# Routed attention and MLP on one core: one ordered list of steps, PV and logits with tokens on partitions, batch 0 in two rounds

## The chip, the cores and the metric

The kernel runs on one core of a Trainium2 chip. The core has five engines with instruction streams of their own: TensorE (PE in the profile; its weight loads are PEld), VectorE (DVE), ScalarE (ACT), GpSimd (POOL) and SyncE (SP), and 16 DMA engines which all queues share. The metric is the device time of one execution in microseconds. Every engine takes its instructions in the order in which they are written, so an instruction that waits holds everything behind it on that engine.

## The reference, cut to what matters

```
B, H, S, D = 4, 8, 768, 64            # 16 clusters; MLP 512 -> 2048 -> 512
q_assign = argmax(q_n @ c_n.T)        # q, k and centroids normalized; per head
k_assign = argmax(k_n @ c_n.T)
scores   = q @ k.T / 8, set to -1e9 where q_assign != k_assign
attn     = softmax(scores)            # over keys
x        = (attn @ v), heads side by side: 3072 tokens x 512
h        = x @ w_in                   # 3072 x 2048
out      = (h * sigmoid(h)) @ w_out   # 3072 x 512
```

A token attends only to keys whose nearest centroid is its own. The length of q or k doesn't change its argmax, so only the centroids are normalized in the kernel. Inputs and output are float32.

## The kernel before, in words

One head is one (batch, head) pair, 32 in all. A head passes through these stages:

- **Load** (`load_qk`, `load_v`): q, k and v, 192 KB each, over SP's queue. Token p*6+j lies on partition p, so each partition reads 1536 bytes in one piece.
- **Split** (`hi` L90, `lo` L96, both DVE): q and k times 128 as a float16 high half and a float16 remainder, side by side in `hl`.
- **Turn** (`xpose` L106): one DMA transpose of twelve 128x128 tiles into `ab`: 64 rows of high half and 64 rows of remainder, tokens along the free side.
- **Cluster logits** (`logits` L116): the centroids are the weights, 32 columns wide, `ab` the moving operand, 384 columns; four matmuls for four column groups of the array, and four more for the centroids' remainder.
- **Argmax** (`am_t` L126, `am_max` L133 and L135, `am_back` L142): transposed in 32x32 blocks on DVE, maximum, one-hot, transposed back.
- **Codes** (`codes` L151, L153, DVE): the one-hot, times 16384, is written over 16 of the remainder rows of `ab`, for keys less 16384. A score matmul over 80 rows then adds zero for equal clusters and a large negative number otherwise.
- **Scores** (`qk_mm` L162, L163) and **exponential** (`exp` L169, ACT): per 128 keys two matmuls, 512 and 256 queries, and one exponential over 768 into `P`, keys on partitions.
- **PV** (`pv_mm` L177): v and 64 columns of ones are the weights (`vts`, cast on POOL, L82), `P` the moving operand, 384 queries at a time, summed over six key tiles in `pO`. The result has head dimensions on partitions, and the ones give the softmax denominators on the other 64.
- **Normalize**: `evac` (L186, DVE) copies `pO` to `osb`; the denominators are sent over SP as `zt`, inverted (`recip` L196), sent to DRAM (`rzd`), and read back broadcast over 64 partitions (`rzb`); `norm` (L213, POOL) multiplies into `xts`, the transposed input of the MLP.

The MLP takes half a batch (384 tokens) at a time: 16 up units of four matmuls with `win_s` as weights (`unit_a` L232), tanh on ACT (L236), (tanh+1)*h on DVE (L237); then three down units of 16 matmuls with 512 columns (`unit_b` L271), an output copy (L276, DVE) and a store (L277). It needs x of all eight heads of its batch. The last batch goes through `unit_aa` (L251, L259, L261), where two halves share one bank pair and one tanh.

The order is written out by hand: a loop over heads and six key tiles, in which the work of neighbouring heads stands at fixed places (scores of the next tile, PV and normalizing of the heads before, loads five and six heads ahead). MLP units of the batch before are put between at fixed places, four up units and one down unit per head. The MLP weights come over POOL's queue, one piece every second head from head 2 on, behind a small copy (`pace`). What the last heads leave over runs behind the loop.

Of the kernel before, what the change touches and what calls it, by code (L numbers as in the profile page):

```python
# [14 lines left out]


@with_exitstack
def kernel(
# [19 lines left out]
    NBH = B * H  # L38
    HALF = S // 2
    assert D == 64 and DM == H * D and S == 768 and HC == 16 and H == 8  # L40
# [4 lines left out]
    NV = 8  # L45

    ctx.enter_context(tc.manual_schedule())

    const = ctx.enter_context(tc.tile_pool(name="const", bufs=1))
    drpool = ctx.enter_context(tc.tile_pool(name="drpool", bufs=1, space=bass.MemoryType.DRAM))  # L50
    mp = ctx.enter_context(tc.tile_pool(name="mp", bufs=1))
    ps = ctx.enter_context(tc.tile_pool(name="ps", bufs=1, space=bass.MemoryType.PSUM))
# [3 lines left out]
    xts = [const.tile([128, NT], f16, name=f"xt{r}") for r in range(NR)]  # L56
    vts = [const.tile([128, NJ, 128], f16, name=f"vt{n}") for n in range(NV)]
    stk = const.tile([128, H, 32], f16, name="stk")
    ckl = const.tile([128, H, 32], f16, name="ckl")
    ohp = [const.tile([128, 12, 32], f16, name=f"oh{n}") for n in range(2)]  # L60
    pace = const.tile([128, 1], f32, name="pace")

    nat, hls, abs_, psLs, LTs, mxs, ohs, Ps, pOs, osbs, zts, rzds, rzbs, pst = ({} for _ in range(14))

    def per_head(f):
        return lambda i, *a: f(i, *a) if 0 <= i < NBH else None

    @per_head
    def load_qk(i):
        b, h = divmod(i, H)  # L70
        qk = mp.tile([128, 2, NJ * D], f32, name="qk", bufs=3)
        nc.sync.dma_start(qk[:, 0, :], q[b, h].rearrange("(p j) d -> p (j d)", j=NJ))
        nc.sync.dma_start(qk[:, 1, :], k[b, h].rearrange("(p j) d -> p (j d)", j=NJ))
        nat[i] = qk

    @per_head
    def load_v(i):
        b, h = divmod(i, H)
        vn = mp.tile([128, NJ, D], f32, name="vn", bufs=3)
        nc.sync.dma_start(vn, v[b, h].rearrange("(p j) d -> p j d", j=NJ))  # L80
        lo = 0 if i % 2 == 0 else 64
        nc.gpsimd.tensor_copy(vts[i % NV][:, :, lo : lo + D], vn)  # L82

    @per_head
    def hi(i, t=slice(0, 2)):
        if i not in hls:
            hls[i] = mp.tile([128, 2 * NJ, 2, D], f16, name="hl", bufs=3)
        hl = hls[i].rearrange("p (t j) c d -> p t j c d", t=2)
        src = nat[i].rearrange("p t (j d) -> p t j d", d=D)
        nc.vector.tensor_scalar(out=hl[:, t, :, 0, :], in0=src[:, t], scalar1=QS, scalar2=None, op0=ALU.mult)  # L90

    @per_head
    def lo(i, t=slice(0, 2)):
        hl = hls[i].rearrange("p (t j) c d -> p t j c d", t=2)
        src = nat[i].rearrange("p t (j d) -> p t j d", d=D)
        nc.vector.scalar_tensor_tensor(  # L96
            out=hl[:, t, :, 1, :], in0=src[:, t], scalar=QS, in1=hl[:, t, :, 0, :], op0=ALU.mult, op1=ALU.subtract
        )

    @per_head  # L100
    def xpose(i, parts=1):
        hl = hls.pop(i)
        ab = mp.tile([128, 2 * NJ, 128], f16, name="ab", bufs=5)
        n = 2 * NJ // parts
        for t in range(parts):
            nc.sync.dma_start_transpose(ab[:, t * n : t * n + n, :], hl[:, t * n : t * n + n].rearrange("p n c d -> p (n c d)"))  # L106
        abs_[i] = ab

    @per_head
    def logits(i):  # L110
        h = i % H
        ab = abs_[i]
        psL = ps.tile([128, HALF], f32, name="psL", tag="mm", bufs=3)
        for w, st in ((stk, True), (ckl, False)):
            for g in range(4):
                nc.tensor.matmul(  # L116
                    psL[32 * g : 32 * g + 32, :], w[:, h, :],
                    ab[:, 3 * g : 3 * g + 3, :].rearrange("p n c -> p (n c)"),
                    start=st, stop=not st,
                )  # L120
        psLs[i] = psL

    @per_head
    def am_t(i):
        LT = mp.tile([128, 12, 32], f32, name="LT", bufs=2)
        nc.vector.transpose(LT.rearrange("p n c -> p (n c)"), psLs.pop(i))  # L126
        LTs[i] = LT

    @per_head
    def am_max(i):  # L130
        LT = LTs.pop(i)
        mx = mp.tile([128, 12], f32, name="mx", bufs=2)
        nc.vector.tensor_reduce(out=mx, in_=LT[:, :, 0:HC], axis=AX.X, op=ALU.max)  # L133
        oh = ohp[i % 2]
        nc.vector.tensor_tensor(  # L135
            out=oh[:, :, 0:HC], in0=LT[:, :, 0:HC], in1=mx.unsqueeze(2).to_broadcast([128, 12, HC]), op=ALU.is_ge
        )

    @per_head
    def am_back(i):  # L140
        ohT = mp.tile([128, HALF], f16, name="ohT", bufs=2)
        nc.vector.transpose(ohT, ohp[i % 2].rearrange("p n c -> p (n c)"))  # L142
        ohs[i] = ohT
# [74 lines left out]
    gts = {}  # L218
    late = []

    def flush():
        while late:
            late.pop(0)()
# [281 lines left out]
```

## Time and profile before

| | us |
|---|---|
| median of 3 runs | 397.43 (392.53 to 397.45) |
| the profiled execution's own time, from first instruction to last (its span) | 395.2 |
| PE busy | 334.0 (85%) |
| DVE busy | 264.4 (67%) |
| ACT busy | 203.8 (52%) |
| POOL busy | 99.0 (25%) |
| mean granted TensorE clock | 0.965 of full |

Busy time is time in which an engine has at least one instruction running. For PE it counts the depth of the pipeline too: matmuls overlap, and the distance between their starts tells what one costs. In lists of groups, the columns are line, engine, operation, output and inputs with shapes, count, busy time in us, mean duration of one in ns, and idle time of the engine ahead of it with what ended it. In timelines the first two columns are start and duration in us; a merged entry has its count behind an x. In the 40 slices each digit is a busy share in tenths of 9.88 us.

### The profile page before, as it was taken

Reading aid. Unit: us, or ns where it says so; the run is one execution under the profiler, and the core shown is the slowest. Engines: PE = TensorE matmul, PEld = TensorE weight load, DVE = VectorE, ACT = ScalarE, POOL = GpSimd, SP = SyncE. Lnnn points to the kernel's source line nnn. Section 1 sums busy time; section 2 is a strip of 40 time slices with the busy share of each in tenths; the row PEclk is TensorE's granted clock in tenths of the full one; section 3 lists DMA queues with packets and bytes.
Section 4 is the critical chain, followed back from the end, with each engine's and each line's share of the span. In section 5 each row is a group of like instructions: output and inputs, shape, how many; then the busy total and the mean of one; then the engine's idle time right before and its main releaser. Section 6 shows DMA issues by size and latency. Waiting matters only on the chain.

```text
span 395.2 us, 5664 instructions
## 1 busy us (share of the span) xinstructions
PE 334.0 (85%) x1921; PEld 167.8 (42%) x1921; DVE 264.4 (67%) x590; ACT 203.8 (52%) x310; POOL 99.0 (25%) x148
## 2 busy tenths in 40 slices
PE   0539868977598799997999899979999999977995
PEld 0114433433254455553555455445555545443442
DVE  5959967876479977794788877786766345256421
ACT  4237746854376755573666666555657524044300
POOL 3110135454343222223221402260223105000000
PEclk9999978888599999999999999999999999999999
DMA  5695899999979835572555555544311103200022
GB/s 141 172 269 114 188 202 225 186 213 227 128 138 190 207 87 134 133 176 74 148 147 148 122 148 147 143 85 89 88 48 23 47 27 88 80 2 0 0 81 80
DMA packets 82125, 48.84 MB, mean 124 GB/s; under 512 B 62128, under 2 KB 76464, under 8 KB 82096
## 3 DMA queue, kind: packets, MB, share of 16 engines
q1 hardware_dynamic: 79408, 44.29, 46.6%
q0 software_dynamic: 2688, 4.19, 7.2%
q8 instruction: 15, 0.25, 0.3%
q14 instruction: 14, 0.11, 0.1%
HBM read 33.59 MB, written 6.39 MB: 101 GB/s over the span
## 4 chain that ended last, share of the span: by engine, by line
PE 61%; DVE 15%; DMA 12%; ACT 4%; issue 3%; POOL 2%; SPq 2%; ACTq 0%; POOLq 0%; DVEq 0%
PE po L271 21%; PE ph L232 13%; PE pO L177 12%; PE pS L162 7%; DMA vn<-in_v_dram 4%; PE pS L163 3%; PE phs L251 3%; DMA qk<-in_k_dram 3%; DVE osb L186 2%; DMA rzb<-rzd 2%; DMA zt<-osb 2%; DVE gt L261 2%; DVE gt L237 2%; PE psL L116 2%; DVE hl L90 1%
## 5 line engine op out<-in xcount | busy, mean ns | idle before, releaser
L169 ACT ACTIVATE P<-pS 128x768 f16<-128x768 f32 x192 | 148.1, 809 | 37.4 <-PE pS L163 37.2
L177 PE MATMUL pO<-P,vt 128*128 128x384 f16 x384 | 89.1, 344 | 14.0 <-DVE osb L186 13.9
L236 ACT ACTIVATE tn<-ph 128x384 f32<-128x384 f32 x96 | 47.2, 491 | 101.3 <-PE ph L232 96.2
L162 PE MATMUL pS<-ab 80*128 80x512 f16 x192 | 78.8, 410 | 15.5 <-DVE ab L153 9.2
L232 PE MATMUL ph<-xt,win_s 128*128 128x384 f16 x384 | 78.5, 328 | 9.8 <-POOL xt L213 9.8
L271 PE MATMUL po<-wout_s,gt 128*128 128x512 f16 x384 | 85.7, 379 | 0.0
L213 POOL TENSOR_TENSOR xt<-osb,rzb 64x384 f16<-64x384 f32 x64 | 65.1, 1035 | 49.7 <-DMA rzb<-rzd 48.7
L237 DVE SCALAR_TENSOR_TENSOR gt<-tn,ph 128x384 f16<-128x384 f32 x96 | 53.0, 553 | 35.8 <-ACT tn L236 34.0
L82 POOL CAST vt<-vn 128x384 f16<-128x384 f32 x32 | 18.0, 563 | 180.2 <-DMA vn<-in_v_dram 149.6
L177 PEld LDWEIGHTS <-vt 128*128 128x128 f16 x384 | 37.6, 101 | 58.9 <-issue 39.2
L271 PEld LDWEIGHTS <-gt 128*128 128x128 f16 x384 | 37.5, 98 | 43.6
L163 PE MATMUL pS<-ab 80*128 80x256 f16 x192 | 55.6, 289 | 0.0
L276 DVE TENSOR_SCALAR ot<-po 128x512 f32<-128x512 f32 x24 | 16.6, 692 | 52.3 <-PE po L271 52.3
L232 PEld LDWEIGHTS <-win_s 128*128 128x128 f16 x384 | 37.4, 97 | 26.7 <-issue 1.2
L186 DVE COPY osb<-pO 128x384 f32<-128x384 f32 x64 | 35.3, 551 | 3.2 <-PE pO L177 2.9
L96 DVE SCALAR_TENSOR_TENSOR hl<-qk,hl 128x768 f16<-128x768 f32 (+1 forms) x33 | 33.1, 1002 | 0.2
L162 PEld LDWEIGHTS <-ab 80*128 80x128 f16 x192 | 19.8, 103 | 29.0 <-DVE ab L153 10.3
L163 PEld LDWEIGHTS <-ab 80*128 80x128 f16 x192 | 19.8, 103 | 24.5 <-issue 12.8
L251 PE MATMUL phs<-xt,win_s 128*128 128x384 f16 x128 | 22.2, 327 | 5.2 <-DVE gt L261 5.2
L259 ACT ACTIVATE tn<-phs 128x768 f32<-128x768 f32 x16 | 13.0, 811 | 25.0 <-PE phs L251 25.0
L90 DVE TENSOR_SCALAR hl<-qk 128x768 f16<-128x768 f32 (+1 forms) x33 | 19.1, 580 | 8.7 <-DMA qk<-in_k_dram 5.5
L261 DVE SCALAR_TENSOR_TENSOR gt<-tn,phs 128x384 f16<-128x384 f32 x32 | 16.3, 551 | 12.1 <-ACT tn L259 12.1
(45 smaller groups left out, 175.7 us busy)
## 6 DMA issues: line engine op xcount, KB each, us to landing
qk<-in_q_dram SPq DMA_DIRECT2D x32, 192.0 KB, 3.4
qk<-in_k_dram SPq DMA_DIRECT2D x32, 192.0 KB, 3.2
vn<-in_v_dram SPq DMA_DIRECT2D x32, 192.0 KB, 3.7
rzb<-rzd SPq DMA_DIRECT2D x32, 192.0 KB, 3.9
out_dram<-ot SPq DMA_DIRECT2D x24, 256.0 KB, 2.2
win_s<-in_moe_w_in_dram POOLq DMA_DIRECT2D x4, 512.0 KB, 7.9
wout_s<-in_moe_w_out_dram POOLq DMA_DIRECT2D x4, 512.0 KB, 7.5
ab<-hl SPq DMA_TRANSPOSE x33, 3.8
```

The source lines that it names most:

```text
L96: nc.vector.scalar_tensor_tensor(out=hl[:, t, :, 1, :], in0=src[:, t], scalar=QS, in1=hl[:, t, :, 0, :], op0=ALU.mult, op1=ALU.subtract)
L162: nc.tensor.matmul(pS[:, 0:512], lhsT, ab[0:80, 0:4, :].rearrange("p n c -> p (n c)"), start=True, stop=True)
L163: nc.tensor.matmul(pS[:, 512:768], lhsT, ab[0:80, 4:6, :].rearrange("p n c -> p (n c)"), start=True, stop=True)
L169: nc.scalar.activation(out=P, in_=pst.pop((i, j))[:, 0:S], func=AF.Exp, bias=0.0, scale=ESC)
L177: nc.tensor.matmul(pOs[i], vts[i % NV][:, j, :], Ps[i, j][:, c * HALF : c * HALF + HALF], start=(j == 0), stop=(j == NJ - 1))
L186: nc.vector.tensor_copy(osb[:, c * HALF : c * HALF + HALF], pOs.pop(i))
L213: nc.gpsimd.tensor_tensor(out=xts[h // 2][o : o + 64, b * S + c * HALF : b * S + c * HALF + HALF], in0=osbs[i][o : o + 64, cs], in1=rzbs[i ...
L232: nc.tensor.matmul(ph, win_s[:, r, ts(fb, 128)], xts[r][:, T0 : T0 + HALF], start=(r == 0), stop=(r == NR - 1))
L236: nc.scalar.activation(out=tn, in_=ph, func=AF.Tanh, bias=0.0, scale=0.5)
L237: nc.vector.scalar_tensor_tensor(out=gt[:, fb, :], in0=tn, scalar=1.0, in1=ph, op0=ALU.add, op1=ALU.mult)
L251: nc.tensor.matmul(phs[:, 512 * c : 512 * c + HALF], win_s[:, r, ts(fb, 128)], xts[r][:, T0 : T0 + HALF], start=(r == 0), stop=(r == NR - 1),)
L271: nc.tensor.matmul(po, gt[:, fc, ts(t, 128)], wout_s[:, fc, :], start=(fc == 0), stop=(fc == NFB - 1))
```

## The change

The kernel is rewritten. Every piece of work becomes a step with an engine, an assumed duration, the steps it comes after, the buffers that it uses and a priority. `Plan.order` runs through all steps with the assumed durations, takes at each turn the step that can start first (the lower key where two can), gives out buffers, and so fixes one order; the kernel is then written out in it.

- **PV** (`attention`, `pv`): `P` is the weights, 128 queries at a time, and v the moving operand: 65 columns, 64 of v and a 2.0 whose product is twice the denominator, or 96 for odd heads. A head has 36 such matmuls where it had 12. Queries now lie on partitions, so the reciprocal and the multiply (DVE) read `pO` directly, and `zt`, `rzd`, `rzb`, `evac` and POOL's `norm` are gone. The result `xn` of two heads is turned into `xt` by a DMA transpose, or on PE with a copy on DVE for batch 0's first round and the last pairs of a batch.
- **Logits** (`part`, `logits`): 128 tokens of `ab` are the weights, the centroids (high half and remainder) the moving operand, 96 columns, or twice 16 in batch 0's first round. Tokens lie on partitions, so the argmax needs no first transposition: sum of the parts, maximum, difference, two marks, one transposition.
- **Codes**: four DMA transfers per part from `ohT` into `ab`, 64-byte pieces; on DVE and ACT for the first two parts only.
- **High halves**: on POOL, the very first on ACT.
- **Batch 0**: its K, V and the first half of its Q are loaded and prepared by pairs of heads (first and second pair turned on PE), eight heads of 384 queries run, then the second half of Q, and eight heads of 384 again. The other batches have whole heads. Loads are of two heads in one transfer.
- **MLP**: halves as before, 16 units of one bank each; tanh for one half at a time throughout; output copies on ACT; factors of one half are folded into the 2.0. After the last exponential the four banks of the scores join the MLP's two.
- **Weights**: `win_s` by blocks of 512 columns, each of the eight transfers held back to an assumed time in the plan.
- **Centroids**: the root on POOL with its power function, where ACT's root and two correction steps on DVE stood.

The written order runs all of batch 0's first round ahead of the first up unit, and all 16 up units of the first half ahead of batch 1's first scores; the MLP's steps have the lowest priority and fill what attention leaves.

```diff
-    def logits(i):
-        for w, st in ((stk, True), (ckl, False)):
-            for g in range(4):
-                nc.tensor.matmul(
-                    psL[32 * g : 32 * g + 32, :], w[:, h, :],
-                    ab[:, 3 * g : 3 * g + 3, :].rearrange("p n c -> p (n c)"),
+                    w = T["ab"][A.i][:, a0 + t, :]
+                    if twin:
+                        nc.tensor.matmul(pL[:, HC * t : HC * t + HC], w, stk[:, hh, 0:HC], start=True, stop=False, ...)
+                        nc.tensor.matmul(pL[:, HC * t : HC * t + HC], w, stk[:, hh, HC : 2 * HC], start=False, stop=True, ...)
+                    else:
+                        nc.tensor.matmul(pL[:, 32 * t : 32 * t + WN], w, stk[:, hh, :], start=True, stop=True)
...
-        nc.vector.tensor_scalar(out=dst, in0=ohT[32 * g : 32 * g + HC, :], scalar1=OHV, ...)
+                if place == "DMA":
+                    nc.sync.dma_start(dst, src)
...
-            nc.tensor.matmul(
-                pOs[i], vts[i % NV][:, j, :], Ps[i, j][:, c * HALF : c * HALF + HALF], start=(j == 0), stop=(j == NJ - 1)
-            )
+                    nn = (D + 1) if h % 2 == 0 else WN
+                    nc.tensor.matmul(
+                        pO[:, (D + 1) * t : (D + 1) * t + nn], w, vt[:, VW * j : VW * j + nn],
+                        start=(j == 0), stop=(j == NJ - 1), skip_group_check=True,
+                    )
...
-        nc.sync.dma_start(zt, osb[zr : zr + 1, :].rearrange("o (p c) -> o p c", c=NJ))
-        nc.vector.reciprocal(rz, zts.pop(i))
-        nc.sync.dma_start(rzd.rearrange("(p c) -> p c", c=NJ), rz)
-        nc.sync.dma_start(rzb[o : o + 64, :], rzds.pop(i).unsqueeze(0).to_broadcast([64, S]))
-        nc.gpsimd.tensor_tensor(out=xts[...], in0=osbs[i][...], in1=rzbs[i][...], op=ALU.mult)
+            nc.vector.reciprocal(rz, pO[...][:, :, D])
+            nc.vector.tensor_tensor(out=xn[...], in0=pO[...][:, :, 0:D], in1=rz.to_broadcast(...), op=ALU.mult)
...
+    for place in range(H * (B + 1)):
+        n, h = divmod(place, H)
+        if n == 0:
+            attention(0, h, 0, HJ, 20 * place, "DVE")
+        elif n == 1:
+            attention(0, h, HJ, NJ, 20 * place, "DVE" if h >= 6 else "DMA")
+        else:
+            attention(n - 1, h, 0, NJ, 20 * place, "DVE" if h == H - 1 else "DMA")
+    for b in range(B):
+        mlp(b, 0, 200 * b, lambda t: "ACT")
+        mlp(b, 1, 200 * b + 100, lambda t: "ACT")
+    exps[-1].adds = (pools["M"], [2, 3, 4, 5])
+    for s in plan.order():
+        s.fn()
```

1010 lines of the change are left out of this document (645 added, 365 removed).

## Prediction

> **What bounds the kernel now.** I read the 40 slices first, then busy time by stage.
>
> ```profile
> PE   0539868977598799997999899979999999977995
> DMA  5695899999979835572555555544311103200022
> ```
> ```profile
> core 0: us, PE busy (x) PEld busy (x) DVE busy (x) ACT busy (x) POOL busy (x), PEclk, DMA share, GB/s
> 0.00:50.00 50.00, 27.72 (x157) 11.70 (x157) 39.03 (x97) 25.84 (x35) 9.09 (x24) 1.00 0.74 176
> 50.00:110.00 60.00, 44.52 (x232) 20.73 (x225) 39.53 (x94) 32.09 (x44) 27.61 (x37) 0.77 1.07 199
> 110.00:320.00 210.00, 195.87 (x1199) 103.05 (x1197) 154.47 (x342) 127.48 (x207) 56.41 (x81) 1.00 0.49 117
> 320.00:395.20 75.20, 65.90 (x345) 32.37 (x342) 31.39 (x58) 18.38 (x27) 5.85 (x6) 1.00 0.14 47
> ```
>
> There are two regimes. Until about 110 us the DMA engines are full (share 0.74, then 1.07) and the granted clock is 0.77; afterwards PE is full and DMA is half idle. Busy time overstates PE, because matmuls overlap, so I take what one really costs from the distance between starts in a dense stretch (timeline of PE):
>
> ```profile
> 201.72 0.27 PE L163 MATMUL pS<-ab 80*128 80x256 f16 x1
> 201.93 0.35 PE L116 MATMUL psL<-ab,stk 128*32 128x384 f16 x4
> ...
> 202.37 0.66 PE L177 MATMUL pO<-P,vt 128*128 128x384 f16 x3
> ...
> 203.27 0.81 PE L232 MATMUL ph<-xt,win_s 128*128 128x384 f16 x4
> 203.92 0.65 PE L177 MATMUL pO<-P,vt 128*128 128x384 f16 x3
> 204.41 0.38 PE L162 MATMUL pS<-ab 80*128 80x512 f16 x1
> 204.63 0.27 PE L163 MATMUL pS<-ab 80*128 80x256 f16 x1
> 204.74 3.62 PE L271 MATMUL po<-wout_s,gt 128*128 128x512 f16 x16
> 208.19 0.38 PE L162 MATMUL pS<-ab 80*128 80x512 f16 x1
> ```
>
> From these starts: a 384-column matmul 0.65/4 = 0.162 us (0.42 ns a column), a score pair 0.33, a 512-column one 3.45/16 = 0.216. The eight logits matmuls take 0.65 from 201.72 to 202.37, less 0.11 for the 256 columns ahead of them: 0.54. PE's work is then scores 192 x 0.33 = 63.4, up 512 x 0.162 = 82.9, down 384 x 0.216 = 82.9, PV 384 x 0.162 = 62.2, logits 32 x 0.54 = 17.3: **309 us** of the span of 395.2. So 86 us are idle. Where? These are the first rows (0 to 110) of L162, L177, L232 and L116, by stage:
>
> ```profile
> 0.00:110.00 110.00, 31.97 (x69) 7.93 (x70) 0.88 0.92 189
> 0.00:110.00 110.00, 33.16 (x126) 13.53 (x126) 0.88 0.92 189
> 0.00:110.00 110.00, 3.79 (x12) 1.56 (x12) 0.88 0.92 189
> 0.00:110.00 110.00, 8.54 (x104) 1.95 (x104) 0.88 0.92 189
> ```
>
> 69 x 0.33 + 138 x 0.162 + 13 x 0.54 = 52 us of work in 110: **58 us of the idle time lie there**, since no MLP can run until batch 0 is done. The other 28 are spread over 285 us. What holds batch 0 is in the chain that ended last:
>
> ```profile
> 47.22 7.59 DMA zt<-osb
> ```
>
> A 3 KB transfer took 7.59 us in a full queue, and DVE stood behind it.
>
> **The change part by part.** Counts come from the written order of each engine.
>
> *PE: PV and logits.* 384 PV matmuls of 384 columns become 1152 with P as the weights: 576 of 65 columns, 576 of 96. Logits become 312 of 96 columns and 144 of 16; 70 transposes of 128 columns come in. No row shows such a short pair (load, then matmul), so it is bounded. Below: columns alone, 27, 41 and 7 ns. Above: each 128x128 load hides behind a 0.11 us, 256-column matmul (204.63 to 204.74), so at most 107 ns. Between them:
>
> ```profile
> 201.92 0.10 PEld L116 LDWEIGHTS <-stk 128*32 128x32 f16 x4 [0.32 <-issue]
> ...
> 202.36 0.28 PEld L177 LDWEIGHTS <-vt 128*128 128x128 f16 x3 [0.32 <-issue]
> ```
> ```profile
> L177 PEld LDWEIGHTS <-vt 128*128 128x128 f16 x384 | 37.6, 101 | 58.9 <-issue 39.2 <-POOL xt L213 0.3
> ...
> L116 PEld LDWEIGHTS <-stk 128*32 128x32 f16 x128 | 3.8, 94 | 14.4 <-issue 13.6 <-DVE stk L351 0.7
> ```
>
> Four loads fit into 0.10 us though each lasts 94 ns, and 128 columns last only 7 ns longer than 32. The matmul at 202.37 starts 0.01 after its own load. So most of the 98 ns is latency that overlaps. I take columns plus about 12 to 20 ns: 42 ns (65), 52 (96), 30 (16), 65 (128). Sum: 24.2 + 30.0 + 16.2 + 4.3 + 4.6 = 79 us, against 62.2 + 17.3 = 79.5 now. **PE's work stays at 308 us**; at the bounds it is 22 lower or 101 higher.
>
> The Trainium skill ("TensorE: Matmul & The Clock Gate", Part 3, the paragraph on what overlaps) says that a weight load overlaps running matmuls only when the row group differs. This trace disagrees: L232's loads use all 128 rows, as its matmuls do, and the cadence stays 0.162 us, which is what 384 columns take.
>
> *Denominators.* The chain zt, rzd, rzb (96 transfers, one behind DVE at 47.22), the evacuation and POOL's normalizing go; 40 reciprocals and 40 multiplies on DVE straight from PSUM come.
>
> ```profile
> L213 POOL TENSOR_TENSOR xt<-osb,rzb 64x384 f16<-64x384 f32 x64 | 65.1, 1035 | 49.7 <-DMA rzb<-rzd 48.7
> L186 DVE COPY osb<-pO 128x384 f32<-128x384 f32 x64 | 35.3, 551 | 3.2 <-PE pO L177 2.9
> L153 DVE TENSOR_SCALAR ab<-ohT 16x384 f16<-16x384 f16 x64 | 19.4, 303 | 0.9
> L151 DVE TENSOR_SCALAR ab<-ohT 16x384 f16<-16x384 f16 x64 | 19.0, 297 | 1.5
> L82 POOL CAST vt<-vn 128x384 f16<-128x384 f32 x32 | 18.0, 563 | 180.2 <-DMA vn<-in_v_dram 149.6 <-PE pS L163 24.2 <-PE ph L232 6.5
> L276 DVE TENSOR_SCALAR ot<-po 128x512 f32<-128x512 f32 x24 | 16.6, 692 | 52.3 <-PE po L271 52.3
> L135 DVE TENSOR_TENSOR oh<-LT,mx 128x192 f16<-128x192 f32 x32 | 14.8, 463 | 1.1
> ...
> L196 DVE RECIPROCAL rz<-zt 128x6 f32<-128x6 f32 x32 | 5.9, 184 | 8.0 <-DMA zt<-osb 8.0
> ```
>
> The 384-element multiply lies between 551 ns (L186, same size from PSUM) and 2 x 463 (L135, a broadcast operand); with 0.2 for the reciprocal that is 30 to 45 us on DVE against 35.3 + 5.9 removed: even. *Codes* leave DVE (19.4 + 19.0) for 124 SP transfers. *High halves* go to POOL, two casts of L82's size per head: 32 x 1.13 = 36 us for the 65.1 it loses. *Output copies* (16.6) go to ACT, which has about 190 us free. The argmax gains two short operations, about 0.4 us a head. DVE ends near 230 us, no engine but PE near the span. On SP the codes' issues wait for DVE's transpose, and loads stand behind them; these loads are asked for five places ahead (some 40 us), which hides it.
>
> *Codes on the DMA engines.* 366 tiles x 64 pieces of 64 bytes.
>
> ```profile
> q1 hardware_dynamic: 79408, 44.29, 46.6%
> q0 software_dynamic: 2688, 4.19, 7.2%
> ```
>
> q1's mean packet costs 0.466 x 16 x 395.2 / 79408 = 37 ns; the new ones lie between nothing and that, 0 to 54 us of all engines over the run, for 96 removed transfers with 6 MB of rzb. I take them as even.
>
> *Batch 0 in two rounds.* All K, V and half of Q, then 24 exponentials instead of 48, and the first MLP half can start. In the new order all 64 up-matmuls of that half stand ahead of batch 1's first scores, together with 96 scores, 288 PV, 204 logits matmuls and 49 transposes: 50 us of PE work. Call the time of those scores T.
> ```profile
> 16.14 0.81 ACT L169 ACTIVATE P<-pS 128x768 f16<-128x768 f32 x1 [7.90 <-PE pS L163]
> ```
> ```profile
> L169 ACT ACTIVATE P<-pS 128x768 f16<-128x768 f32 x192 | 148.1, 809 | 37.4 <-PE pS L163 37.2
> ...
> L236 ACT ACTIVATE tn<-ph 128x384 f32<-128x384 f32 x96 | 47.2, 491 | 101.3 <-PE ph L232 96.2 <-DVE gt L237 3.4 <-DVE osb L186 1.1
> ```
> - From below: ACT has 48 exponentials (148.1 / 192 = 0.77 us each), 16 tanh (0.49) and copies of about 3 us, 48 us in all. Its first exponential starts at 16.1 now, and I take 14 (two table loads and the transposes' transit go, POOL's power function comes): T is at least 62.
> - By DMA: weights 7.2% = 28.5 us; q1 46.6% = 184 us, 5.8 a head. About ten heads' worth of traffic stands ahead: 58 + 28.5 = 86 us. The four w_out quarters (14 us) aren't needed by then: 72.
> - From above: 110, as now.
>
> I take **T = 76**. From there PE has 144 score pairs, 864 PV, 252 logits, 196 up, 192 down: 175 us of attention with filler, then 252 up and 192 down with no attention, 83 us.
>
> *Tail.* The up-matmuls of the last batch now wait for their bank:
>
> ```profile
> PE phs L251 <- DVE gt L261: 5.2, 7, 1.0
> ```
> ```profile
> 387.73 3.40 PE L271 MATMUL po<-wout_s,gt 128*128 128x512 f16 x15
> ```
> Six banks instead of two pairs remove that: 5 us, already in the sum since I count the tail at full rate.
>
> **Sum**: 76 + 175 + idle 14 (8% of 175: now 17 of the 210 us from 110 to 320, where PE's work by the same cadences is 193) + 83 + 4 from the last matmul to the end, as now (387.73 + 3.40 to 395.2), = 352 us span. The median of the runs lies 2.2 above the profiled span (397.4 to 395.2), so **354 us**.
>
> **The rivals.**
> 1. *A load holds the array* (slower). If half of a load's 98 ns kept the array from streaming, a pair costs 49 + about 34 = 83 ns, and 1678 pairs cost 139 instead of 79 us: 354 + 60 = 414. At the bound of 107 ns: 455. It overtakes the gain from about 73 ns a pair on. For: no row shows short pairs. Against: four loads in 0.10 us. The Trainium skill ("TensorE: Matmul & The Clock Gate", Back-to-back issue gap) gives about 81 ns for a stream of such pairs at 128 columns; by an estimate from that page 1678 pairs cost 136 us and the time would be about 411.
> 2. *The queue still holds batch 0.* Packets of 64 bytes, a weight stream beside the loads and PE's fixed order, which cannot use filler while a score waits for its codes, keep T at 110: 388. For: 1.07 share now. The Trainium skill ("DMA: Bandwidth & Descriptors", Specifications) wants 512 bytes for line rate, since smaller writes are read and modified first; no row here separates that cost.
> 3. *T is ACT's bound*, 62, and the filler leaves 8 us idle: 334.
> 4. *The two rounds don't do what they say*: POOL issues the weights behind its high halves and casts, w_in arrives late, the first up-matmuls stand at PE's head. Same place and price as 2.
>
> **How the numbers follow.** Forecast (340 to 372) 0.58; rival 3 and better 0.13; rivals 2 and 4 0.15, a third of it within 2% of now; rival 1 0.11, rest 0.03. A difference of 2% (8 us) is about what runs of this kernel, 392.5 to 397.5, can tell. Range: 330 (rival 3 with some of the lower pair bound) to 392 (rival 2). Faster by over 2%: 0.81; within: 0.07; slower: 0.12.
>
> **What would show it.** In the profile after: starts of PV matmuls 40 to 55 ns apart (step 1; 80 or more is rival 1); first up-matmul near 50 us and first score of batch 1 near 76; DMA share below 0.7 after 110 us; granted clock under 0.9 only in the first 80 us; no wait of DVE for a transfer of denominators; some 80 us of MLP alone at the end with PE full; POOL and DVE under 70%. The prediction is wrong if PE stands at scores waiting for codes after 110 us (DMA or DVE late), or if short pairs run over 65 ns.

## The result, and the profile after

The changed kernel takes **380.84 us** (median of 4 runs, 379.38 to 384.62), against 396.48 for the kernel before beside it: a ratio of **0.965, 95% interval 0.958 to 0.973**. It is faster, by 16 us where the forecast of 354 meant 42. The profiled execution's span is 382.6 us, against 395.2. Ratios leave disturbed runs out; for one kernel below (the plan with 3 us) the ratio is therefore lower than its median alone would give.

The 40 slices of the page of after (one slice is 9.57 us), then busy time by stage:

```profile
PE   2740668889989989998798998988999999998995
...
PEclk9955558699999999999899998999999999999999
DMA  7599594289596949548856784838020010100101
```
```profile
core 0: us, PE busy (x) PEld busy (x) DVE busy (x) ACT busy (x) POOL busy (x), PEclk, DMA share, GB/s
0.00:100.00 100.00, 63.30 (x702) 43.98 (x703) 53.01 (x146) 49.73 (x75) 31.51 (x68) 0.76 0.77 153
100.00:292.00 192.00, 174.28 (x1821) 110.94 (x1822) 114.00 (x278) 134.21 (x207) 30.90 (x60) 0.98 0.64 137
292.00:382.60 90.60, 82.70 (x439) 42.49 (x436) 32.00 (x64) 34.01 (x74) 0.00 (x0) 1.00 0.10 35
```

The three stages are batch 0, attention with MLP work between, and the MLP alone. In the first the clock granted to TensorE is 0.76 on average by the row, and 0.5 in slices 3 to 6; the DMA engines are 0.77 busy. In the second the DMA share is 0.64. DVE, which had 264.4 us, has 199.0 by the page, POOL 62.4 instead of 99.0, ACT 217.9 instead of 203.8.

The clock column has a gap: up to the first change that the profile records it counts the clock as full. The distances between starts say otherwise. Timeline of PE in the kernel before:

```profile
30.54 1.17 PE L177 MATMUL pO<-P,vt 128*128 128x384 f16 x3
31.50 0.63 PE L162 MATMUL pS<-ab 80*128 80x512 f16 x1
...
36.11 0.65 PE L177 MATMUL pO<-P,vt 128*128 128x384 f16 x3
36.60 0.38 PE L162 MATMUL pS<-ab 80*128 80x512 f16 x1
```

Three matmuls of 384 columns take 0.96 us at 30.5 us and 0.49 us at 36.1 us: 0.32 and 0.16 us each. So TensorE ran at half pace early in the kernel before, where the page shows 9 in every slice of PEclk up to there and the prediction read a clock of 1.00 for the first 50 us. In after the same happens: transposes of 128 columns start 107 ns apart until 15.6 us and 55 ns apart from 16.9 us on. The 0.76 is therefore too high for the first stage.

**What a short pair costs.** Timeline of PE in after: a run of 16-column logits that alternate between two lines, and three pieces of a dense stretch, all at full clock.

```profile
19.25 0.17 PE L473 MATMUL pL<-stk,ab 128*128 128x16 f16 x1
...
20.13 0.17 PE L477 MATMUL pL<-stk,ab 128*128 128x16 f16 x1
...
114.08 1.71 PE L638 MATMUL pO<-vt,P 128*128 128x96 f16 x36
115.62 0.38 PE L595 MATMUL pS<-ab 80*128 80x512 f16 x1
...
118.33 0.67 PE L482 MATMUL pL<-stk,ab 128*128 128x96 f16 x12
118.84 0.38 PE L595 MATMUL pS<-ab 80*128 80x512 f16 x1
...
122.81 0.89 PE L638 MATMUL pO<-vt,P 128*128 128x65 f16 x24
123.54 0.38 PE L595 MATMUL pS<-ab 80*128 80x512 f16 x1
```

36 pairs of 96 columns take 1.54 us, 43 ns each; 24 of 65 columns 0.73 us, 30 ns; 12 logits 0.51, 42 ns. That is the columns at 0.42 ns and 2 or 3 ns more: every load, though it lasts about 100 ns, is hidden. From the first to the last of 36 matmuls of 16 columns 0.88 us pass, 25 ns each, so going from 65 to 16 columns saves little. All PV and logits matmuls come to 576 x 0.030 + 576 x 0.043 + 312 x 0.042 + 144 x 0.025 = 59 us, and about 5 for the transposes: **64 us** where I had 79.

The Trainium skill ("TensorE: Matmul & The Clock Gate") has two figures for this. Its section "Back-to-back issue gap" gives about 81 ns for a stream of load and matmul pairs at 128 columns; this trace disagrees, with 43 ns at 96, and so does that of the run without weights below, in which twelve transposes of 128 columns start 55 ns apart (20.84 to 21.50 us). Its Part 1 ("Wait — 56ns, not 53.3ns?") says that starts are never closer than about 25 ns however few the columns; the 25 ns here agree.

**The groups that answer to those shown of before** (line, engine, operation, names, shapes, count, busy us, mean ns, idle ahead and what ended it; the second fence keeps shapes apart; the third is the queues' part of the page):

```profile
L638 PE MATMUL pO<-vt,P 128*128 128x96 f16 (+1 forms) x1152 | 56.0, 206 | 1.8 <-ACT P L612 0.9
...
L482 PE MATMUL pL<-stk,ab 128*128 128x96 f16 x312 | 19.0, 212 | 16.7 <-DMA ab<-hl 13.7
...
L651 DVE RECIPROCAL rz<-pO 128x6 f32<-128x6 f32 (+1 forms) x40 | 7.3, 184 | 40.2 <-PE pO L638 39.8
```
```profile
L656 DVE TENSOR_TENSOR xn<-pO,rz 128x384 f16<-128x384 f32 x24 | 13.4, 558 | 0.8
```
```profile
q1 hardware_dynamic: 96848, 40.05, 46.9%
q0 software_dynamic: 4224, 4.19, 6.8%
```

DVE no longer waits for a transfer of denominators: the reciprocal waits for PE. But the logits now wait, and for the DMA transposes: 13.7 us. In the chain that ended last, these transposes have the largest single share:

```profile
DMA ab<-hl 16%; PE pM L745 10%; PE pS L745 9%; PE pM L716 7%; PE pO L638 6%; PE pS L716 6%; PE pS L595 4%; PE pL L482 4%; DMA nv<-in_v_dram 4%; SPq L430 3%; SPq L555 3%; DVE gq L727 3%; DVE hl L417 3%; PE pS L599 2%; ACT P L612 1%
```

The waits (engine, tile and line, what it waited for: total, times, longest):

```profile
ACT P L614 <- PE pS L605: 39.9, 21, 22.7
...
PE pL L482 <- DMA ab<-hl: 13.7, 13, 3.0
PE pL L473 <- DMA ab<-hl: 13.6, 1, 13.6
...
PE pS L745 <- ACT ot L758: 2.7, 4, 0.7
```

The same for PE alone, from 100 to 292 us:

```profile
PE pL L482 <- DMA ab<-hl: 9.0, 11, 2.0
```

One stop of 13.6 us in batch 0, two more (4.6 us) in its second round, and eleven of at most 2.0 us (9.0 in all) behind it. The big one, by the timelines of POOL, SP, PE and ACT:

```profile
18.34 3.20 POOL L774 DMA_DIRECT2D win_s<-in_moe_w_in_dram  x4
...
19.66 18.08 SPq L430 DMA_TRANSPOSE ab<-hl  x2
...
37.85 0.19 PE L473 MATMUL pL<-stk,ab 128*128 128x16 f16 x1 [13.59 <-DMA ab<-hl]
...
44.45 1.51 ACT L614 ACTIVATE P<-pS 128x768 f16<-128x768 f32 x2 [22.72 <-PE pS L605]
```
```profile
20.00:60.00 40.00, 18.16 (x196) 12.10 (x193) 12.11 (x34) 9.61 (x13) 6.57 (x11) 0.50 0.99 152
```

The four w_in pieces are issued from 18.3 us on, and the transposes of batch 0's third and fourth pairs from 19.7 on. SP is held by these two for 18.08 us; PE's next instruction in its order is a logits matmul on their result; ACT gets no score for 22.7 us. From 20 to 60 us the DMA share is 0.99 and the clock 0.50. The first up-matmul and the first scores of batch 1 come accordingly:

```profile
74.72 1.05 PE L716 MATMUL pM<-xt,win_s 128*128 128x384 f16 x5
...
99.95 0.38 PE L595 MATMUL pS<-ab 80*128 80x512 f16 x1
```

So T, the time of batch 1's first scores, is **100.0** instead of 76.

**The balance.** I took every matmul of the trace at its columns and 2 ns as work, and the rest of the distance to the next start as idle (a stretch at half clock counts as half idle):

| | forecast | measured |
|---|---|---|
| T | 76 | 100.0 (43 work, the rest idle or lost to the clock) |
| work from T to the end of attention | 175 | 163 |
| idle there | 14 | 29 (14 of it ahead of logits, L482, whatever they waited for; 5 ahead of up-matmuls, L716) |
| MLP alone, work | 83 | 81 |
| MLP alone, idle | 0 | 5.5 |
| last matmul to the end | 4 | 4 |
| span | 352 | 382.6 |

PE's work is 43 + 163 + 81 = 287 us, where before it was 309; idle time is 382.6 - 287 = 96, where before it was 86. **What the change gained is about 22 us of matmul work, which I had called even; the idle time, which I had expected to shrink, grew by 10.**

### The profile page after: what moved, and what is told of

It reads as the page before. It is cut to its first block, busy times and chain, and to the rows that moved or that the text cites. A ratio compares the mean times of both kernels' runs of the same rounds, so it can differ in the third digit from the quotient of the medians.

```text
span 382.6 us, 7732 instructions
## 1 busy us (share of the span) xinstructions
PE 320.3 (84%) x2958; PEld 197.4 (52%) x2958; DVE 199.0 (52%) x486; ACT 217.9 (57%) x355; POOL 62.4 (16%) x128
## 3 DMA queue, kind: packets, MB, share of 16 engines
q1 hardware_dynamic: 96848, 40.05, 46.9%
## 4 chain that ended last, share of the span: by engine, by line
PE 49%; DMA 22%; DVE 11%; SPq 7%; ACT 4%; issue 3%; POOL 2%; DVEq 0%; POOLq 0%; ACTq 0%
DMA ab<-hl 16%; PE pM L745 10%; PE pS L745 9%; PE pM L716 7%; PE pO L638 6%; PE pS L716 6%; PE pS L595 4%; PE pL L482 4%; DMA nv<-in_v_dram 4%; SPq L430 3%; SPq L555 3%; DVE gq L727 3%; DVE hl L417 3%; PE pS L599 2%; ACT P L612 1%
## 5 line engine op out<-in xcount | busy, mean ns | idle before, releaser
L716 PE MATMUL pM<-xt,win_s 128*128 128x384 f16 x352 | 69.0, 329 | 4.3 <-DVE gq L727 4.3
L716 PEld LDWEIGHTS <-win_s 128*128 128x128 f16 x512 | 50.2, 98 | 41.0 <-issue 8.6
L745 PEld LDWEIGHTS <-gq 128*128 128x128 f16 x384 | 37.6, 98 | 46.4 <-issue 7.0
L727 DVE SCALAR_TENSOR_TENSOR gq<-tn,pM 128x384 f16<-128x384 f32 x88 | 46.0, 545 | 29.8 <-ACT tn L722 29.7
L638 PE MATMUL pO<-vt,P 128*128 128x96 f16 (+1 forms) x1152 | 56.0, 206 | 1.8 <-ACT P L612 0.9
L745 PE MATMUL pM<-wout_s,gq 128*128 128x512 f16 x224 | 57.0, 383 | 0.4 <-DVE gq L727 0.4
L638 PEld LDWEIGHTS <-P 128*128 128x128 f16 x1152 | 51.9, 102 | 9.5 <-issue 1.5
L722 ACT ACTIVATE tn<-pM 128x384 f32<-128x384 f32 x88 | 41.8, 502 | 5.1 <-PE pM L716 4.7
L745 PE MATMUL pS<-wout_s,gq 128*128 128x512 f16 x160 | 36.0, 379 | 3.9 <-ACT ot L758 2.7
L605 PE MATMUL pS<-ab 80*128 80x384 f16 x96 | 28.1, 412 | 7.5 <-ACT ab L557 2.6
L482 PE MATMUL pL<-stk,ab 128*128 128x96 f16 x312 | 19.0, 212 | 16.7 <-DMA ab<-hl 13.7
L716 PE MATMUL pS<-xt,win_s 128*128 128x384 f16 x160 | 28.6, 326 | 0.3 <-ACT tn L722 0.2
L482 PEld LDWEIGHTS <-ab 128*128 128x128 f16 x312 | 15.7, 101 | 23.4 <-DMA ab<-hl 18.9
```

What stands on the lines that cost most here:

```text
L482: nc.tensor.matmul(pL[:, 32 * t : 32 * t + WN], w, stk[:, hh, :], start=True, stop=True)
L605: nc.tensor.matmul(pS[sb.i][:, 512 * i : 512 * i + HALF], ab[0:80, kt[2 * s + i], :], ab[0:80, qt : qt + HJ, :].rearrange("p n c -> p (n c ...
L638: nc.tensor.matmul(pO[:, (D + 1) * t : (D + 1) * t + nn], w, vt[:, VW * j : VW * j + nn], start=(j == 0), stop=(j == NJ - 1), skip_group_c ...
L716: nc.tensor.matmul(banks[bank.i][:, 0:HALF], win_s[:, r, ts(fb, 128)], T["xt"][xtb[b].i][:, r, T0 : T0 + HALF], start=(r == 0), stop=(r == ...
L722: nc.scalar.activation(out=T["tn"][tn.i], in_=banks[bank.i][:, 0:HALF], func=AF.Tanh, bias=0.0, scale=1.0)
L727: nc.vector.scalar_tensor_tensor(out=T["gq"][g.i][:, fb % 4, :], in0=T["tn"][tn.i], scalar=1.0, in1=banks[bank.i][:, 0:HALF], op0=ALU.add, ...
```

## The experiments

My theory after this trace: two things undid the forecast, both through DMA transposes. The weights and the transposes meet on the DMA engines and stop batch 0; and the plan believes that a transpose can be used too soon, so PE's order has logits standing too early. Rivals: the two rounds themselves cost; PE's work alone sets the time; the chain of batch 0 is long whatever DMA does. Each edit is to the changed kernel unless another is named.

### Weights behind the transposes of pairs three and four

```
+    for s in steps:
+        if s in weights and s.start is not None and not getattr(mark, "gone", False):
+            continue
         s.fn()
...
+        if s is mark:                       # the transposes turns[0, 3, 0]
+            mark.gone = True
+            gate()                          # POOL copy of a piece of their result
+            for w in weights:               # the ones held back
...
```

> Edit: POOL copies one element per partition out of the turned tile of batch 0's fourth pair ahead of the first w_in transfer, so that all eight weight transfers start only when the DMA transposes of pairs three and four have landed; nothing else moves. Theory A (the weight stream takes the DMA engines from these transposes): ACT's stop of 22.7 us before its seventh exponential falls below 10, the two transposes are issued within 8 us instead of 18.1, time falls by 8 to 16 us, to 365 to 373. Rival B (two transposes of 18 tiles are this slow by themselves): the stop stays above 17 us, time within 3 us of 381.

Measured: **381.5 us** (378.9 to 383.2), ratio 0.960 (0.953 to 0.968), T 95.7. Timelines of SP and ACT:

```profile
19.47 5.39 SPq L431 DMA_TRANSPOSE ab<-hl  x2
39.47 8.82 SPq L431 DMA_TRANSPOSE ab<-hl  x2
```
```profile
31.20 1.51 ACT L616 ACTIVATE P<-pS 128x768 f16<-128x768 f32 x2 [9.90 <-PE pS L607]
...
56.24 1.51 ACT L616 ACTIVATE P<-pS 128x768 f16<-128x768 f32 x2 [9.73 <-PE pS L607]
```

The same two transposes hold SP for 5.39 us instead of 18.08, and the stop falls from 22.7 to 9.9 us: the weights were what stretched them. Most of the 9.9 us that are left pass before the first weight transfer is issued, at 27.1 us, so they have another cause. And the next pair of transposes, at 39.5, now runs beside the weights, and a second stop of 9.7 us appears. The stop and the transposes did what theory A said; the time did not, it hardly moves. The Trainium skill ("DMA: Bandwidth & Descriptors", Issuing engines are not separate DMA queues) says that transfers from all queues run on the same 16 engines and interleave; this agrees, since a stream from POOL's queue more than tripled the time of SP's transfers.

### Weights behind the second round's transposes

The same edit with `mark = turns[0, 3, 18][0]` and the copy taken from that part's tile.

> Edit: the same copy, but from the turned tile of the second half of Q of the fourth pair, so the weights start when all DMA transposes of batch 0 have landed. Theory A: the first stop is short as in the run before and the PE waits for second-half transposes (3.2, 1.9, 1.9 us) shrink too, but the up-matmuls wait for w_in: the first one no earlier than 10 us after the copy. Time 360 to 378. Rival B: first stop unchanged at over 17 us, time 385 or more, since the weights come later on top.

Measured: **383.3 us** (380.3 to 384.4), ratio 0.963 (0.956 to 0.970), T 99.4.

```profile
73.52 11.05 SPq L431 DMA_TRANSPOSE ab<-hl  x1
...
92.66 1.51 ACT L616 ACTIVATE P<-pS 128x768 f16<-128x768 f32 x2 [10.21 <-PE pS L607]
```

(The first row is of SP, the second of ACT.) Now a transpose of batch 1 meets the weights: 11.05 us for one. The first stop is again about 10 us (10.29), long before the weights, which are issued from 54.9 us on. The time lies above the theory's 360 to 378. The lengthened stop follows the weights to wherever they are put, as long as a DMA transpose is needed soon.

### No weights

```
-                nc.gpsimd.dma_start(
-                    win_s[:, :, ts(n, 512)], moe_w_in.rearrange(...)[:, :, ts(n, 512)]
-                )
+                nc.gpsimd.memset(win_s[:, :, ts(n, 512)], 0.01)
...
-                nc.gpsimd.dma_start(wout_s[:, 4 * n : 4 * n + 4, :], ...)
+                nc.gpsimd.memset(wout_s[:, 4 * n : 4 * n + 4, :], 0.01)
```

> Edit: the eight weight transfers are replaced by POOL memsets of a constant, so the MLP works with constant weights; all else is the same. It leaves the weights' load out, to price it. Theory A': no stop over 10 us in batch 0, first score of batch 1 at 70 to 80, time 352 to 364 (17 to 29 less than 381). Rival C (PE's half clock and the fixed order cost the time between 45 and 75 us whatever the weights do): first score of batch 1 no earlier than 88, time over 368.

Measured: **370.3 us** (369.3 to 372.3), ratio 0.932 (0.925 to 0.940), T 84.8. Timelines of SP and ACT, and PE's waits:

```profile
20.25 5.42 SPq L430 DMA_TRANSPOSE ab<-hl  x2
```
```profile
33.61 1.51 ACT L614 ACTIVATE P<-pS 128x768 f16<-128x768 f32 x2 [11.53 <-PE pS L605]
```
```profile
PE pL L482 <- DMA ab<-hl: 11.7, 12, 2.4
```

The weights cost this kernel 15 us of T and 11 us of time. Neither expectation is met: the stop is 11.5 us, T lies between the two, and the time is above 368, as rival C said. T is still 9 above the forecast, and the waits of logits for transposes from 100 us on are almost unchanged (8.8 us where they were 9.0): they are the second cause, and it has nothing to do with the weights.

The edit has a cost of its own, here and in the last run without weights. POOL fills four pieces for 7 us where it had issued transfers for 3.2 us, and DVE's marks, ahead of the codes, stand beside the fill (timelines of POOL and DVE in that other run):

```profile
18.19 7.03 POOL L774 MEMSET win_s<- 128x2048 f16 x4
```
```profile
22.54 2.80 DVE L535 TENSOR_SCALAR oh<-Df 128x192 f16<-128x192 f32 x1
...
28.59 0.26 DVE L535 TENSOR_SCALAR oh<-Df 128x192 f16<-128x192 f32 x1
```

The same operation takes 2.80 us beside the fill and 0.26 without it; in the run of this section two of them take 2.75 and 2.25 us. So both runs may price the weights too low, by up to 4.5 and 2.5 us.

### First round of batch 0 turned on PE

```
-            hi_eng="POOL", turn={"k": "ACT", "q": "DVE"} if p == 1 else "DMA", twin=True,
+            hi_eng="POOL", turn={"k": "ACT", "q": "DVE"}, twin=True,
```

> Edit: pairs three and four of batch 0's first round are turned on PE with copies on ACT and DVE, as pair two is; the weight stream is left where it is. Theory A' (the weight stream starves whichever DMA transposes are in flight, and PE's fixed order then stands still): the stop of 22.7 us shrinks to under 9 since nothing there needs a DMA transpose, the second round's transposes still meet the rest of the weights; first score of batch 1 at 82 to 92 instead of 100, time 366 to 376. Rival B' (the sum of all DMA work ahead of that point sets it, 77 us of engine time by the windows, and 7 of it go): first score of batch 1 at 93 to 97, time 375 to 380.

Measured: **377.5 us** (373.6 to 378.4), ratio 0.948 (0.940 to 0.956), T 93.4. PE's waits:

```profile
PE pL L482 <- DMA ab<-hl: 16.4, 15, 5.7
PE pS L605 <- DMA ab<-ohT: 9.8, 2, 9.3
```

The stop at the logits of the first round goes; in its place PE stands 9.3 us for codes, which are DMA transfers too, under the same weights. Two thirds of the stop come back one step later (9.3 of 13.6 us). T and the time both lie in the range of rival B', the sum of DMA work, so this run doesn't decide for the theory. Later runs decide against that rival: with batch 0 turned on PE the DMA engines' share up to T is 0.79 of 83.8 us with the weights and 0.46 of 82.0 without, 66 and 38 us of work for nearly the same T.

### The plan's delay for a transpose

In `Plan.order`, one constant: how long after its transfer a DMA transpose may be used.

```
-                s.end = max(wire[s.eng], t + s.w) + (1000 if turned else 1200)
+                s.end = max(wire[s.eng], t + s.w) + (3000 if turned else 1200)
```

> Edit: the plan assumes 3.0 us instead of 1.0 from the end of a transpose's transfer to its use, so logits matmuls are written later in PE's order. If PE's idle time after 100 us (29 us, half of it ahead of logits) comes from an order that takes transposes for too quick: waits of logits for transposes fall from 13.7 to under 6 us and time by 5 to 10 us. If the waits only move to scores (codes come later too): time within 3 us of 381.

Measured: **364.5 us** (359.7 to 371.0), ratio 0.910 (0.900 to 0.918), T 96.9. PE's waits of the profiled execution (span 357.7):

```profile
PE pL L482 <- DMA ab<-hl: 2.2, 3, 1.5
```

By the constants that stand around this line, the plan had reckoned 0.3 + 12 x 0.195 + 1.0 = 3.6 us from the issue of a 12-tile transpose to its use; the trace of after has a median of 3.9 us to the landing alone, over all of them, and 3.7 to 6.8 us for those of 12 tiles from 100 us on (issues by group: count, us to landing):

```profile
ab<-hl SPq DMA_TRANSPOSE x30, 3.9
```

With the new constant, 13.7 us of waits became 2.2 (from 100 us on, 9.0 became 2.2), and the time from T to the end fell from 282.6 to 260.8 us. By the balance above, idle time after T until attention ends is 15 us instead of 29, and 11 of these 14 lie ahead of logits; the MLP's own stretch has 3.5 us less idle time, and 4.4 us more of matmul work lie before T. The matmuls come to the same 287 us; PE has other work standing ahead of each logits matmul. The gain is above the 5 to 10 us that I expected.

### Both, in all of batch 0

The constant of 3000, the edit of the first round, and the second round's parts turned on PE too:

```
-                0, p, [("q", 0, HJ, NJ), ("q", 1, HJ, NJ)], 18, 40 + 20 * p, hi_eng="POOL", pace=s
+                0, p, [("q", 0, HJ, NJ), ("q", 1, HJ, NJ)], 18, 40 + 20 * p, hi_eng="POOL", turn={"k": "ACT", "q": "DVE"}, pace=s
```

> Edit: all turning of batch 0 but its first-half results' last step on PE (first and second round), and the plan assumes 3 us from transfer to use of a DMA transpose as in the earlier run that gave 364. Theory A': neither weights nor transposes meet in batch 0, first score of batch 1 at 75 to 85, waits of logits for transposes stay under 5 us, time 342 to 354. Rival B': 358 to 364, no better than the latency alone.

Measured: **353.3 us** (353.1 to 354.7), ratio 0.890 (0.884 to 0.895), T 86.7. PE's largest wait:

```profile
PE pS L605 <- DMA nq<-in_q_dram: 8.9, 1, 8.9
```

By the row this wait is for a load of queries; what is on PE just there is a score, which needs codes as well. The next run has the same wait and puts it down to the codes. Either is a transfer under the weights again. The time lies in the theory's range, T just outside it.

### Batch 0 on PE with the old delay

The same without the 3000.

> Edit: all turning of batch 0's parts on PE, the assumed latency left at 1 us; it parts the 353 us run into its two edits. If both work on different stages and add up: the latency is worth 16 (381 to 364), so this one lies at 366 to 372, with first score of batch 1 at 84 to 90 and over 10 us of waits of logits for DMA transposes left after it.

Measured: **370.6 us** (368.0 to 371.4), ratio 0.933 (0.927 to 0.940), T 85.1.

```profile
PE pL L482 <- DMA ab<-hl: 13.9, 13, 2.1
PE pS L605 <- DMA ab<-ohT: 9.0, 1, 9.0
```

By the ratios, taken of 396 us, turning batch 0 on PE alone is worth 13 us and the delay alone 22, and both together 30 (by the medians 10, 16 and 27.5). So they nearly add, one mostly before T and one behind it, as expected.

### A longer delay

Both, with 5000 instead of 3000.

> Edit: the kernel of the 353 us run with 5 us instead of 3 from transfer to use of a DMA transpose in the plan. If PE's remaining waits after 87 us (15 us of idle, 7 of it scores that wait for codes) come from too short an assumption still: 346 to 351. If not: 352 to 357, since more lead takes buffers and puts filler out of place.

Measured: **355.1 us** (353.9 to 355.5), ratio 0.895 (0.888 to 0.901). A longer delay than 3 us gains nothing more.

### Both, and the weights behind the third pair's codes

```
+    mark = max(puts[0, 2, 0], key=steps.index)   # last codes transfer of the third pair
...
+        if s is mark:
+            gone = True
+            nc.gpsimd.tensor_copy(pace[64:80], T["ab"][abuf[0, 2].i][64:80, 0, 127:128])
...
```

> Edit: the kernel of the 353 us run, and POOL copies one element per partition out of the codes of batch 0's third pair ahead of the first weight transfer, so that the weights (from 18 us on there) start only when these codes have landed. Theory A'' (the same stream of weights delays the small codes transfers and second-half loads, PE stands 9 us at 27 us): that wait falls under 3 us, the first score of batch 1 moves from 86.7 to 76 to 82, time 345 to 350. Rival: the weights' 28 us of DMA work only move behind, as they did in the run with the weights after the transposes; time 351 to 356.

Measured: **350.05 us** (349.0 to 353.1), ratio **0.884 (0.877 to 0.891)**, T 83.8; the best kernel here, by 8% over the changed one (350.05 / 380.84 = 0.919). The wait of 8.9 us is gone, and only 3 us of it are gained; T stays just above the 76 to 82 that were expected. The longest stop of ACT in batch 0 is 4.3 us for a score.

### The same without weights

The kernel of "Both, in all of batch 0" with the weights replaced by a constant as above.

> As e8_all_batch0_on_PE_3us (353.3 us, first scores of batch 1 at 86.7), but the weights are not loaded: GpSimd fills them with a constant, so the output is not the reference's. It asks what holds batch 0 once neither DMA transposes nor the weight stream are there. Theory 1, the DMA engines are all that keep T from the forecast: T 75 to 79 us, time 341 to 346. Theory 2, the plan's own chain does (stretches of half clock, PE's fixed order, DVE's work on the splits and codes): T 81 to 85, no stop over 4 us, time 347 to 351, about that of e9_e8_weights_after_codes (350.1).

Measured: **350.3 us** (348.9 to 350.8), ratio 0.886 (0.879 to 0.894), T 82.0. With no transposes of q and k by DMA in batch 0 and no weight stream, T is no nearer to 76 than that. The windows up to T:

```profile
12.00:26.00 14.00, 10.86 (x161) 8.56 (x160) 13.54 (x24) 10.10 (x14) 14.00 (x14) 0.98 0.27 88
26.00:42.00 16.00, 13.51 (x144) 9.82 (x144) 8.88 (x23) 6.11 (x9) 6.46 (x7) 0.50 0.24 41
42.00:82.00 40.00, 38.14 (x445) 25.67 (x443) 32.51 (x92) 32.26 (x51) 8.14 (x13) 0.99 0.51 124
```

From 42 us on PE is full. Ahead of that DVE is busy 13.54 of 14 us while it splits and codes the next heads, and then PE works 16 us at a clock of 0.50 with the DMA engines at 0.24. (The 0.98 of the first row again counts as full what ran at half pace: transposes of 128 columns start 107 ns apart until 18 us.) Some 2.5 of the 13.54 us are the mark that stands beside POOL's fill; but the kernel of the section before, which has no fill, is alike, with DVE busy 12.97 of the same 14 us and a clock of 0.57 in the 16 us behind. T and the time are those of theory 2. So the weights, well placed, cost little (350.05 with them, 350.3 without, and perhaps 2.5 less without the fill), and the rest of the way to 76 is likely to lie in DVE's stretch and in the half clock behind it. Which of the two sets it was not tried. The matmuls of the 16 us come to 6.5 us at their columns and 2 ns, so I estimate that the half clock adds no more than about that.

### One round in batch 0

All queries of a head at once, as before the change:

```
-    load_q(0, 0, -89, 0, HJ, eng="ACT", hs=(0,))
+    load_q(0, 0, -89, 0, NJ, eng="ACT", hs=(0,))
...
-            attention(0, h, 0, HJ, 20 * place, "DVE")
+            attention(0, h, 0, NJ, 20 * place, "DVE")
...
```

> Edit: batch 0 runs in one round of 768 queries like the other batches, prepared head by head (pairs one and two turned on PE as before); its MLP half then waits for eight whole heads. If the two rounds carry the gain of the change: first up-matmul at 95 or later instead of 75, time 388 to 400. If the gain is in PE's shorter work and the removed denominators alone: 378 to 386. If two rounds cost (more transfers, more waits): under 376.

Measured: **387.0 us** (385.9 to 388.8), ratio 0.975 (0.967 to 0.983). Batch 0's last exponential starts at 94.9 us, against 97.3 with two rounds, so the rounds cost batch 0 about 2 us; they gain some 6 in time by the medians, between the first and the second expectation. The first up-matmul comes at 98.9 us where it came at 74.7, since the first MLP half waits for all of batch 0. The intervals of the two ratios overlap, so the size is rough.

### All heads with 96 columns

```
-                    nn = (D + 1) if h % 2 == 0 else WN
+                    nn = WN
```

> Edit: even heads' PV matmuls take 96 columns as the odd ones do (576 pairs, 29 to 43 ns each by the starts seen so far), 8 us more PE work, 6 of it after the first score of batch 1. If PE's work sets the time after that point: 385 to 389 (4 to 8 more). If PE mostly waits there for something else: within 2 us of 381.

Measured: **385.1 us** (383.8 to 386.0), ratio 0.970 (0.964 to 0.976), T 99.2. 576 pairs become 13 ns longer, 7.5 us of PE work; about 4 show in the time, the lower edge of what was expected if PE's work sets it (the intervals overlap). PE is not the only bound: by the balance, 5.6 us of the added work lie behind T, where the idle time falls from 29 to 25.

## Why the prediction was wrong

The direction held, the size didn't: 354 was forecast, 380.8 measured, inside the range of 330 to 392. By the steps:

1. **"I take T = 76" failed, by 24 us.** The amount of DMA work was estimated well: 0.77 of 100 us is 77, between the 72 and 86 that I gave. What failed is the idea behind it, that the engines' work sets T: the runs above have nearly the same T with 66 and with 38 us of it. The stream of weights (6.8% of 382.6, 26 us of all engines) began to be issued 1.3 us ahead of two transposes for which PE's order had nothing to put in front, and these were held 18.08 us instead of about 5.4. Without weights T is 84.8, with batch 0 turned on PE 85.1 (86.7 with the longer delay), with both 82.0. So some 6 us of the 24 are there with neither. Of the other 18 about 10 come only where weights and DMA transposes meet, since the weights cost 15 us of T beside DMA transposes and 5 without them; the transposes alone account for the last 3. These are single traces, two of them with the fill on POOL, so the split is rough. The lower bound of 62 from ACT was not near in any run.
2. **"Idle 14" after T failed, by 15 us.** I scaled the idle share of the kernel before to an order that I had not seen run. In the new order the plan's own delay decides: from 100 us on, with 1000 the logits stand ahead of their transposes eleven times (9.0 us of PE standing still by the waits), with 3000 three times (2.2), and the idle time is then 15, what I had forecast. By its repair this is the larger loss: that alone gave 22 us by the ratios, that of batch 0 alone 13.
3. **The term of the short pairs was mis-sized, 79 for 64 us**, to the good; that luck hid part of the two misses above. I gave each pair 12 to 20 ns beyond its columns; it has 2 or 3 from 65 columns on, and 25 ns at 16 columns. Of my own bounds the lower one ("columns alone") was nearly right from 65 columns on. "PE's work stays at 308" was therefore wrong: 287 by columns and 2 ns.
4. **"5 us, already in the sum" for the tail** came out at nothing: the up-matmuls' wait for their bank is gone, and the down-matmuls wait for ACT's output copies instead (2.7 us in the waits); 5.5 us stay idle in the MLP's own stretch. Its work, 81 for 83 us, was right.
5. **Taken as even, and rightly:** the codes on the DMA engines (q1 had 46.6%, has 46.9%; the packets of 64 bytes cost 15 us of all engines, where I gave nothing to 54); DMA share under 0.7 after 110 us (0.63); no wait for denominators. DVE came out better than said, 199 us for about 230: its multiply of 384 elements takes 558 ns, at the lower end of the 551 to 926 that I gave, and POOL has 62 for about 70. Neither is near the span.
6. **The signs were looked for in the wrong place.** I named two by which the prediction would be wrong, scores that wait for codes after 110 us and pairs over 65 ns. Neither came: after 110 us PE waits 0.2 us for codes, and pairs cost 30 and 43 ns. The clock of 1.00 that I read for the first 50 us of before is half of that until about 34 us, but the sum doesn't use it.

**The rivals.** Rival 1, a load that holds the array, falls: 30 and 43 ns where it needed 73. Rival 2 is what happened, in part: the weight stream beside the transfers and PE's fixed order, with T at 100 and not 110; its packets of 64 bytes were not needed for it, since the transposes stopped at the logits ahead of any code. Codes under the weights stop PE too (9.3 and 9.0 us in the runs that turn batch 0 on PE). I gave it and rival 4 together 0.15, too little for a stage whose DMA share before was already above 1. Rival 3 falls with T. Rival 4, w_in late, falls: the weights came too early, and in after no up-matmul waits for them. The two rounds do what they say, for roughly 6 us.

The forecast's time was reached by other kernels (353.3 and 350.05), but by another sum: T at 87 and 84 instead of 76, idle time as forecast, and 15 us less for the pairs.

**What stays open:** why T stays at 82 with neither weights nor DMA transposes (DVE's work or the half clock); what part of the weights' price the fill on POOL hides; why a stop of 10 us stays in batch 0 ahead of the weights; and the spread of the kernel with the delay alone, 359.7 to 371.0.

## What to carry to other kernels

In a static order, every transfer needs the delay that it has in the running kernel; here 3.6 us were reckoned to the use where the landing alone took 3.7 to 6.8, and 2 us more in one constant gained some 20 us, spread over waits of which none behind batch 0 is longer than 2.0 us. A bulk load is best issued where nothing short is needed from the DMA engines next: moving it from one short transfer to another moves the stop, taking the transposes away from it, onto TensorE, left 9 us at the next short transfer, and only with the bulk load put behind that one as well was the stop gone. Matmuls whose weights change each time could be priced here at their columns (0.42 ns each) and 2 or 3 ns from 65 columns on, since the loads ahead of them were hidden. And an experiment that takes work off one engine should be looked at for what it puts on another: the fill that stood in for the weights slowed DVE.

## What the runs showed of the hardware that I had not expected

- A 128x128 weight load of about 100 ns is hidden even behind a 65-column matmul: starts 30 ns apart. 16 columns cost 25 ns, hardly less than 65.
- Two DMA transposes take 5.4 us of SP's queue without a weight stream and 18.1 us beside 1 KB packets of a stream from another queue; a single one 11.05 us. The granted TensorE clock stays at 0.50 for 40 us meanwhile, while PE is busy 18 of these 40.
- The same clock of 0.50 was held for 16 us with PE busy 13.5 of 16; it was back in the stretch behind it, in which PE was busy 38 of 40 us (0.99).
- The clock column of a page shows full clock up to the first recorded change, although matmuls of 384 columns started 0.32 us apart there, and 0.16 later.
- A DVE operation of 0.26 us took 2.80 us beside a 7 us fill on POOL.
